# A seventh V tile kept per batch, and each head's gK in the light iteration, in an attention block's backward pass

## Chip, core and metric

One NeuronCore of a Trainium2 chip runs the kernel. The metric is device time in microseconds (us) of one execution. A NeuronCore has five engines that run their own instruction streams: TensorE (PE in the profile; its weight loads are PEld), VectorE (DVE), ScalarE (ACT), GpSimd (POOL) and SyncE (SP). They work on the on-chip memory SBUF (128 partitions) and on the accumulation memory PSUM, which has eight banks here called bank0 to bank7. Transfers between the device memory and SBUF run on 16 DMA engines; they are issued from the queues of SP, ACT and POOL.

## The reference

The reference computes one decode step of a transformer block and the gradients of all its inputs. B = 2 batches, one query each, D = 640, H = 32 heads of 128, a cache of 4096 keys and values per head, and an MLP of width 1728:

```python
q = (layernorm(x) @ wq)                       # 2 x 32 x 128
p = softmax(q . k_cache * 128**-0.5)          # 2 x 32 x 4096
o = p . v_cache
h = x + o @ wo
h2 = h + relu(layernorm(h) @ w1) @ w2
out, vjp = jax.vjp(f, x, k_cache, v_cache, wq, wo, w1, w2)
return out, *vjp(grad_out)
```

The outputs are h2 and the gradients of x, of the two caches (gK and gV, 2 x 32 x 4096 x 128 each) and of the four weight matrices. K, V, gK and gV make up nearly all of the bytes: one head of one of them is 4096 x 128 bf16, 1024 KB, and is held on chip as one tile of 8 KiB a partition.

## The kernel before

**Two passes over 64 (batch, head) pairs.** The first pass (`p1_iter`, L449) takes the pairs in order. It loads K and V of a pair, transposes K on TensorE (`pair_transpose`, L415: four groups of transposes into PSUM, each copied to a tile `t_sb` with the tag "XT"), multiplies by the query (`pair_matvec`, L431), takes the maximum (`rmax`, L559) and its negative on all partitions (`nb`, L505), the exponential (`ep`), and multiplies K by it on VectorE in two halves (`pk_half`, L461). TensorE then forms m = sum of V and pk (`m_part`) and u (`u_part`). The work is pipelined: iteration i does the scores of pair i, the exponentials of pair i-1 and the m products of pair i-2.

The second pass (`p2_iter`, L814) goes through the 64 pairs as "turns". A turn needs V again (called W there): it transposes W (T0 to T3), multiplies by the gradient of o (`dp`), forms gV = p x go on VectorE (two halves, `outer_half`, L806), and then gsp (L822) and gK = gsp x q (two halves). gV and gK are stored from POOL's queue (L871, L850). In the kernel before, a turn's last quarter of dp, its gsp and its gK are made at the start of the next turn.

**Kept V.** The order of the turns (L396) puts the last KEPT[b] heads of a batch first. The V tiles of those heads stay on chip from the first pass, so their turn needs no W load (L398). KEPT is (6, 6): 52 of the 64 turns load W.

**Phases.** The plan (L1091) interleaves the passes. Iterations 0 to 33 do pair 0 to 31 of the first pass. Then the first batch's middle (`middle_gen`, L719: the attention output, the layer norm, the MLP forward and backward, the gradient of o by `go_group`) runs in the background of iterations 34 to 40. From iteration 41 (P2_AT) to 63 the passes are mixed: every other iteration, a "mixed" one, also starts a turn; the one after it, a "light" one, finishes that turn's gV. Turns 0 to 11 are started there, 12 and 13 in iterations 64 and 65, and the rest follow alone, with the second batch's middle and the weight gradients (`fin_gen`, L955, and `gx_gen`, L989) in the background. MIXED and REST (L1139) say behind which of the eight steps of a first-pass iteration a step of the turn is issued. Background work is issued a piece at a time; `slot` says behind which steps a VectorE product of a row (`ttr`, L641) may be issued, at most one each.

**Tiles.** Twelve 8 KiB tiles (NBIG, L80) have homes: "ld" for loads, "g" for gK and gV, later "f" and "q" for the weight gradients. `take` and `give` move them, `share` sets how many each home is to have. The kept V tiles stay in "ld". Between iterations 41 and 45 three tiles move to "g". When the first pass is over its pool is released and two more tiles are added, "ld" gets KEPT[1] + 3 and "g" 5; when the second kept set is done (L1166) "ld" is cut to 5; when all gradients of o are done (`late`) six more tiles come from the space of wo. SP's queue issues the loads of K, V and W in the order of one list, written out ahead, each as soon as a tile in "ld" is free (`pump`, L1116). An instruction that needs a tile waits, on its own engine's queue, for the tile's last users.

**Small buffers that the change touches.** XT has 5 buffers, `rb` (L835) 4, `gsp` and `pp` 3. `xr`, `u4`, `fbc`, `junk` and `hbc` have a place each. The output row (`orow`, L637) has two buffers, used for two rows of the output and two of x's gradient; a row is copied by VectorE and stored from SP's queue.

Of the kernel before, what the change touches and what calls it, by code (L numbers as in the profile page):

```python
# [15 lines left out]
def kernel(  # L16
# [63 lines left out]
    NBIG = 12  # L80
# [71 lines left out]
    neg_ident = const.tile([128, 128], BF16)  # L152
    nc.vector.tensor_scalar(out=neg_ident[:], in0=ident_bf[:], scalar1=-SCALE, scalar2=None, op0=ALU.mult)
# [25 lines left out]
    xr = cols.tile([4 * ND, 128], BF16)  # L179
# [96 lines left out]
    def ln_bwd(gh, xh, rstd, add, dst, nb):  # L276

        def t3(name):
            return small.tile([128, nb, ND], FP32, tag=f"lb_{name}{nb}", bufs=1, name=f"lb_{name}")
# [3 lines left out]
        mm = small.tile([128, 2, nb], FP32, tag=f"lb_mm{nb}", bufs=1, name="lb_mm")  # L283
# [5 lines left out]
        nm = small.tile([128, 2, nb], FP32, tag=f"lb_nm{nb}", bufs=1, name="lb_nm")  # L289
# [32 lines left out]
    pkp = tc.alloc_tile_pool(name="pkp", bufs=1)  # L322
    hot = pkp.tile([128, 2 * H - 1], BF16)
    nc.gpsimd.memset(hot[:], 0.0)
    nc.gpsimd.memset(hot[:, H - 1:H], 1.0)
    es = pkp.tile([128, B, H], FP32)
# [68 lines left out]
    KEPT = (6, 6)  # L395
# [4 lines left out]
    u4 = cols.tile([128, 128], FP32)  # L400
# [14 lines left out]
    def pair_transpose(nat, g, dve=False, busy=0):  # L415
# [8 lines left out]
        t_sb = mats.tile([128, GT // 2, 128], FP32, tag="XT", bufs=5, name="t_sb")  # L424
# [24 lines left out]
    def p1_iter(i, dve_group, busy):  # L449
# [60 lines left out]
        if p is not None:  # L510
            ep = pkp.tile([128, NSC, 2], BF16, tag="ep", bufs=3, name="ep")
            nc.scalar.activation(out=ep[:], in_=p["s"][:, :, None].to_broadcast([128, NSC, 2]),  # L512
                                 func=ACT.Exp, bias=nb[:], scale=SCALE, accum_out=es[:, bp, hp:hp + 1])
# [24 lines left out]
        if p is not None and hp % OG == OG - 1:  # L538

            totp = p["bank"][:, 256:256 + OG]  # L540
            nc.tensor.matmul(totp, lhsT=half_f32, rhs=es[:, bp, hp + 1 - OG:hp + 1], start=True, stop=True)
# [66 lines left out]
    def u_out(b):  # L608

        t = pst([128, H], FP32, "mid", "uc_ps")  # L610
        nc.tensor.matmul(t[:], lhsT=u4[:], rhs=fold[:], start=True, stop=True)
        nc.vector.tensor_tensor(out=Uc[:, b, :], in0=t[:], in1=rt[:, b, :], op=ALU.mult)


# [18 lines left out]
    def store_row(col_bf, n, dst):  # L633
# [3 lines left out]
        r = small.tile([16, 128], BF16, tag="orow", bufs=2, name="orow")  # L637
# [3 lines left out]
    def ttr(in0, in1, acc, width, kc=128, junk=None):  # L641
        if junk is None:
            junk = cols.tile([128, D], BF16, tag="junk", name="junk")
# [14 lines left out]
    def go_group(b, h0, h1, hbc):  # L658
# [4 lines left out]
        for k in range(n):  # L663
            yield from turn()
            ttr(wo_t[:, h0 + k, :], hbc[:], go32[:, k:k + 1], D)
# [25 lines left out]
    def mlp_out():  # L691

        ml32 = small.tile([128, ND, B], FP32, tag="ml32", bufs=1, name="ml32")
# [16 lines left out]
        ml_bf = small.tile([128, ND, B], BF16, tag="ml_bf", bufs=1, name="ml_bf")  # L710
        nc.vector.tensor_copy(out=ml_bf[:], in_=ml32[:])
        y_bf = small.tile([128, B, ND], BF16, tag="y_bf", bufs=1, name="y_bf")
# [6 lines left out]
    def middle_gen(b):  # L719
        if o_next[0] < (b + 1) * H // OG:  # L720
            o_group()
        nc.vector.tensor_reduce(out=u4[:], in_=u_bank[0][:].rearrange("p (s d) -> p d s", s=4),
# [35 lines left out]
        FW = Dff // 3  # L758
        spread_f = bcast_cols(one(ghfc, b), NF, f_kc, fbc)
        have = 0  # L760
        for k in range(3):
            while have < min(Dff, (k + 1) * FW):
                next(spread_f)
                have += 512
# [15 lines left out]
        for h0, h1 in bounds:  # L780
            yield from go_group(b, h0, h1, hbc)
# [3 lines left out]
    def ga_gen():  # L785

        gbc = cols.tile([128, Dff], BF16, tag="fbc", name="gbc")
        for b in range(B):
            yield from bcast_cols(one(gc, b), ND, lambda c: 128, gbc[:, b * D:(b + 1) * D])
        for k in range(NW2):  # L790
# [3 lines left out]
            for c in range(k * FP, min(NF, (k + 1) * FP)):  # L794
                kc = f_kc(c)
                for b in range(B):
                    yield from turn()
                    ttr(t[0:kc, c - k * FP, :], gbc[0:kc, b * D:(b + 1) * D], ga[0:kc, b, c:c + 1], D, kc)
# [15 lines left out]
    def p2_iter(j, busy, act=0):  # L814

        c = S2[j] if j < NP1 else None
        p = S2[j - 1] if j >= 1 else None
        if p is not None:
            bp, hp = turns[j - 1]
            pair_matvec(p["dp"], p.pop("T3"), 3, gom[:, hp, bp, :, :])  # L820
            gsp = small.tile([128, NSC, 2], BF16, tag="gsp", name="gsp")
            nc.vector.scalar_tensor_tensor(  # L822
                out=gsp[:], in0=p["dp"][:, :, None].to_broadcast([128, NSC, 2]), scalar=negdot[:, hp, bp:bp + 1],
                in1=P_bf[:, bp * H + hp, :, None].to_broadcast([128, NSC, 2]), op0=ALU.add, op1=ALU.mult)
        if c is not None:
# [41 lines left out]
        yield  # L867
        outer_half(gV, c["rb"][:, 0:128], c["pp"], 1, act)
# [3 lines left out]
        give(gV)  # L872
        yield

# [114 lines left out]
    def gx_gen(fin):  # L989
# [30 lines left out]
        junk = cols.tile([128, GW], BF16, tag="fbc", name="gxj")  # L1020
        for c in range(ND):
# [4 lines left out]
            for b in range(B):  # L1026
                for k in range(NGW):
                    ttr(t[:, k * GW:(k + 1) * GW], rows[b][:, k * GW:(k + 1) * GW], gxp[:, b, c, k:k + 1], GW, junk=junk)
# [10 lines left out]
        for b in range(B):  # L1039
            gxo = small.tile([128, ND], BF16, tag="gxo", bufs=2, name="gxo")  # L1040
# [99 lines left out]
    REST = {1: 1}  # L1140
# [8 lines left out]
    for n, (i, j) in enumerate(plan):  # L1149
# [16 lines left out]
        elif fin is not None and j >= H + KEPT[1] - 1:  # L1166
            share(ld=5 + more, g=5 + 2 * more, f=3, q=2 + 3 * more)
        if j is not None:
# [4 lines left out]
            g2 = p2_iter(j, 0, 8 if i is None and j <= H else 0)  # L1173
# [32 lines left out]
        for k, _ in enumerate(p1_iter(i, i < H + 1, 0)):  # L1206
# [9 lines left out]
            if i >= P2_AT:  # L1216
                slot[0] = int(k == 6 or (k == 1 and j is None))
# [49 lines left out]
```

## Time and profile before

| | |
|---|---|
| median of 3 runs | 897.68 us (895.79 to 898.74) |
| the profiled execution | 897.56 us, of which the span of instructions is 895.8 us |
| TensorE busy | 739.5 us (83%) |
| VectorE busy | 687.7 us (77%) |
| ScalarE busy | 482.6 us (54%) |
| POOL busy | 202.7 us (23%) |
| bytes moved | 361.84 MB, mean 404 GB/s |
| largest group on VectorE | pk 128 x 1.22 us, gK 128 x 1.23 us, gV 128 x 1.14 us |

The page cuts the span into 40 slices of 22.4 us. In its lines of slices a digit is a busy share in tenths, and GB/s is what the DMA engines moved in that slice. In a row of a group, xN is the number of instructions, followed by the busy time and the mean duration in ns; behind the second bar stands the idle time of the engine just before them and what ended it. In a row of the order of time, the first number is the start in us from the span's start, the second the length, and a bracket gives the idle time before it and what ended it. Matmuls overlap, so their lengths don't add up; TensorE's busy time is no measure of how near it is to its peak.

### The profile page before, as it was taken

To read this page: it belongs to the slowest core of one execution; us is meant where nothing else is said; L and a number is where in the kernel's file an instruction comes from. 1 tells how busy PE (TensorE), PEld (TensorE's weight loads), DVE (VectorE), ACT (ScalarE), POOL (GpSimd) and SP (SyncE) were. 2 spreads that over 40 slices of the span, in tenths; PEclk is the share of its full clock that TensorE was granted. 3 is DMA by queue.
4 is the path that set the end of the run, shared out by engine and by line. 5 is a ranking of instruction groups with operands and counts; after the bars stand their busy time and mean duration, and the time that the engine had idled before them with its cause. 6 is when DMAs were issued, how large, how long until landed. Compare 5 with 4: busy or idle time off the path is not lost.

```text
span 895.8 us, 24578 instructions
## 1 busy us (share of the span) xinstructions
PE 739.5 (83%) x10145; PEld 616.0 (69%) x10145; DVE 687.7 (77%) x1284; ACT 482.6 (54%) x1242; POOL 202.7 (23%) x349
## 2 busy tenths in 40 slices
PE   4999899899997997997977776877878897787593
PEld 4888788788886886886766765665657665564452
DVE  2666788777887786786877897788788679987963
ACT  1444344344554554564645777777556864466372
POOL 1343444343211110010021232222111111111111
PEclk9999999999999899897995556555566855575555
DMA  9999999999879999999999999999999999999997
GB/s 379 425 418 416 417 406 418 425 424 380 311 307 370 377 399 424 424 424 422 399 383 400 422 419 422 419 415 421 417 417 363 425 425 425 425 425 426 425 422 295
DMA packets 56288, 361.84 MB, mean 404 GB/s; under 512 B 5680, under 2 KB 11760, under 8 KB 15472
## 3 DMA queue, kind: packets, MB, share of 16 engines
q1 hardware_dynamic: 34520, 211.13, 57.9%
q0 software_dynamic: 18432, 134.23, 35.9%
q10 hardware_dynamic: 3224, 14.92, 4.0%
q8 instruction: 80, 1.31, 0.5%
q14 instruction: 32, 0.26, 0.1%
HBM read 211.11 MB, written 149.13 MB: 402 GB/s over the span
## 4 chain that ended last, share of the span: by engine, by line
PE 42%; DMA 28%; DVE 14%; ACT 9%; issue 5%; SPq 1%; POOL 0%; ACTq 0%; POOLq 0%; DVEq 0%
PE t_ps L423 18%; DMA Vt<-in_A_v_cache_dram 13%; PE m_ps L457 10%; DMA out_dram<-gK 9%; DVE gV L809 4%; ACT gV L870 3%; PE s_ps L436 3%; PE u_ps L486 3%; ACT t_sb L428 2%; PE dp_ps L436 2%; DVE gK L809 2%; DVE pk L464 2%; PE o_ps L909 2%; DMA out_dram<-gV 2%; DVE junk L644 2%
## 5 line engine op out<-in xcount | busy, mean ns | idle before, releaser
L428 ACT COPY t_sb<-t_ps 128x512 f32<-128x512 f32 x479 | 273.6, 586 | 194.7 <-PE t_ps L423 189.7
L436 PEld LDWEIGHTS <-t_sb 128*128 128x128 bf16 x4096 | 179.4, 102 | 60.5 <-ACT t_sb L428 30.4
L423 PE MATMUL t_ps<-ident_f,Wt 128*128 128x128 f32 x832 | 197.1, 386 | 2.7 <-DMA Wt<-in_A_v_cache_dram 2.4
L457 PE MATMUL m_ps<-pk,Vt 128*128 128x129 bf16 x2048 | 171.9, 222 | 16.6 <-DMA Vt<-in_A_v_cache_dram 16.0
L464 DVE TENSOR_TENSOR pk<-Kt,ep 128x2048 bf16<-128x2048 bf16 x128 | 156.5, 1223 | 33.5 <-PE m_ps L457 15.4
L809 DVE TENSOR_TENSOR gK<-rb,gsp 128x2048 bf16<-128x2048 bf16 x128 | 152.6, 1226 | 15.3 <-DMA out_dram<-gV 13.2
L423 PE MATMUL t_ps<-ident_f,Kt 128*128 128x128 f32 x1024 | 156.0, 285 | 5.7 <-DMA Kt<-in_A_k_cache_dram 5.5
L423 PEld LDWEIGHTS t_ps<-ident_f,Wt 128*128 128x128 f32 x832 | 137.0, 200 | 32.3 <-issue 25.6
L457 PEld LDWEIGHTS <-Vt 128*128 128x128 bf16 x2048 | 125.3, 99 | 47.7 <-issue 28.9
L809 DVE TENSOR_TENSOR gV<-rb,pp 128x2048 bf16<-128x2048 bf16 (+1 forms) x128 | 142.7, 1140 | 10.2 <-DMA out_dram<-gK 8.8
L474 POOL COPY pk<-ep 128x16 bf16<-128x16 bf16 x80 | 84.1, 1053 | 160.8 <-ACT ep L512 86.5
L423 PEld LDWEIGHTS t_ps<-ident_f,Kt 128*128 128x128 f32 x1024 | 113.2, 145 | 9.8 <-PE s_ps L436 4.1
L436 PE MATMUL dp_ps<-gom,t_sb 128*128 128x2 bf16 x2048 | 95.9, 168 | 20.5 <-ACT t_sb L428 20.3
L871 POOL DMA_DIRECT2D out_dram<-gV x64 | 34.2, 534 | 293.2 <-DVE gV L809 173.5
L436 PE MATMUL s_ps<-qm,t_sb 128*128 128x2 bf16 x2048 | 87.4, 164 | 1.5 <-DVE t_sb L426 1.5
L850 POOL DMA_DIRECT2D out_dram<-gK x64 | 34.0, 531 | 227.6 <-DVE gK L809 172.6
L571 ACT CAST MT<-m_ps 128x128 bf16<-128x128 f32 x64 | 17.1, 267 | 105.3 <-PE m_ps L457 105.1
L915 ACT CAST ot<-o_ps 128x512 bf16<-128x512 f32 (+3 forms) x152 | 68.0, 492 | 6.9 <-DMA out_dram<-ot 5.6
L822 DVE SCALAR_TENSOR_TENSOR gsp<-dp_ps,negdot,P_bf 128x64 bf16<-128x64 f32 x64 | 18.0, 281 | 55.8 <-PE dp_ps L436 55.7
L836 ACT ACTIVATE rb<-dp_ps,rt 128x256 bf16<-128x256 f32 x64 | 30.2, 471 | 56.9 <-PE dp_ps L831 56.8
L644 DVE CUSTOM_DVE_ANT_0 junk<-wo_t,hbc 128x640 bf16<-128x640 bf16 x64 | 52.5, 820 | 0.2
L644 DVE CUSTOM_DVE_ANT_0 gxj<-wqs,gqr 128x1024 bf16<-128x1024 bf16 x40 | 48.8, 1219 | 1.4 <-DMA wqs<-in_A_wq_dram 1.2
(200 smaller groups left out, 763.2 us busy)
## 6 DMA issues: line engine op xcount, KB each, us to landing
Kt<-in_A_k_cache_dram SPq DMA_DIRECT2D x64, 1024.0 KB, 16.5
Vt<-in_A_v_cache_dram SPq DMA_DIRECT2D x64, 1024.0 KB, 16.0
out_dram<-gV POOLq DMA_DIRECT2D x64, 1024.0 KB, 13.5
out_dram<-gK POOLq DMA_DIRECT2D x64, 1024.0 KB, 13.7
Wt<-in_A_v_cache_dram SPq DMA_DIRECT2D x52, 1024.0 KB, 12.0
wq_t<-in_A_wq_dram SPq DMA_DIRECT2D x5, 1024.0 KB, 11.9
wo_t<-in_A_wo_dram SPq DMA_DIRECT2D x4, 1280.0 KB, 19.0
wqs<-in_A_wq_dram SPq DMA_DIRECT2D x5, 1024.0 KB, 21.0
```

The costliest lines, as they stand in the source:

```text
L423: nc.tensor.transpose(t_ps[:, j, :], natf[:, 2 * cc:2 * cc + 2, :].rearrange("p c k -> p (c k)"), ident_f[:])
L428: nc.scalar.copy(out=t_sb[:], in_=t_ps[:])
L436: nc.tensor.matmul(dst[:, sc:sc + 2], lhsT=v[:, j, :, par], rhs=vecs[:, par, :], start=(par == 0), stop=(par == 1))
L457: nc.tensor.matmul(r["m"][:, 0:129], lhsT=r["V"][:, sc, :], rhs=r["pk"][sc // HALF][:, sc % HALF, 0:129], start=(sc == 0), stop=(sc == NSC ...
L464: nc.vector.tensor_tensor(out=p["pk"][k][:, :, 0:128].rearrange("p s (a two) -> p s a two", two=2), in0=p["K"][:, sl, :].rearrange("p s (a ...
L474: nc.gpsimd.tensor_copy(out=col, in_=e)
L644: nc.vector.tensor_tensor_reduce(out=junk[0:kc, 0:width], in0=in0, in1=in1, scale=1.0, scalar=0.0, op0=ALU.mult, op1=ALU.add, accum_out=acc)
L809: nc.vector.tensor_tensor(out=pairs_view(dst[:, sl, :]), in0=row.rearrange("p (a two) -> p a two", two=2)[:, None, :, :].to_broadcast([128 ...
L836: nc.scalar.activation(out=rb[:], in_=bank[:, 128:384], func=ACT.Copy, scale=rt[:, b, h:h + 1])
L850: nc.gpsimd.dma_start(out=natural(out_2, bp, hp), in_=gK[:])
L871: nc.gpsimd.dma_start(out=natural(out_3, b, h), in_=gV[:])
L915: nc.scalar.copy(out=ot[0:P, k, n0:n0 + nn], in_=o_ps[0:P, 0:nn])
```

## The change

KEPT becomes (7, 7) and NBIG 13: 14 turns find their V on chip. The space for the thirteenth tile comes from smaller buffers: XT 5 to 4, rb 4 to 3, gsp and pp 3 to 2, orow and other late rows moved to the late pool `fin` (orow with one buffer), and one shared row `wide_row` in place of `u4`, `fbc`, `hbc`, `junk` and the other wide rows. Products whose full result isn't needed write it over P_bf's later heads, or over w1, or into the other half of the wide row. The MLP gradient's row is spread in three pieces of 640, 640 and 448 columns (before 3 x 576). In the mixed phase a turn's last quarter of dp, its gsp and its gK are made in the light iteration that follows the turn's start (`own_gK`) and no longer in the next mixed one. The background products may be issued behind step 1 of the mixed iteration instead of the light one. After the second kept set "g" gets one tile more.

The diff, cut to its core:

```diff
-    NBIG = 12
+    NBIG = 13
...
-    xr = cols.tile([4 * ND, 128], BF16)
+    xr = mats.tile([4 * ND, 128], BF16, tag="XT", bufs=4, name="xr")
...
+        lb = small if nb == 1 else fin
...
-    es = pkp.tile([128, B, H], FP32)
+    es = pkp.tile([128, 2 * OG], FP32)
...
-    KEPT = (6, 6)
+    KEPT = (7, 7)
...
-    u4 = cols.tile([128, 128], FP32)
+    u4 = [None]
...
-        t_sb = mats.tile([128, GT // 2, 128], FP32, tag="XT", bufs=5, name="t_sb")
+        t_sb = mats.tile([128, GT // 2, 128], FP32, tag="XT", bufs=4, name="t_sb")
...
+    def wide_row(name):
+        return cols.tile([128, B * D], BF16, tag="wide_row", name=name)
+
+    def later_heads():
+
+        return P_bf[:, B * H - D // NSC:, :].rearrange("p h s -> p (h s)")
+
+    def spread_some(colsrc, c0, n, kc_of, dst):
+
+        t = pst([128, D], BF16, "bc", "bcb_ps")
+        w = 0
+        for c in range(c0, c0 + n):
+            kc = kc_of(c)
+            nc.tensor.transpose(t[:, w:w + kc], colsrc[0:kc, c:c + 1].to_broadcast([kc, 128]), ident_bf[0:kc, 0:kc])
+            w += kc
+        nc.scalar.copy(out=dst[:, 0:w], in_=t[:, 0:w])
+        return w
...
-        r = small.tile([16, 128], BF16, tag="orow", bufs=2, name="orow")
+        r = fin.tile([16, 128], BF16, tag="orow", bufs=1, name="orow")
...
-        fbc = cols.tile([128, Dff], BF16, tag="fbc", name="fbc")
+        fbc = wide_row("fbc")
...
+        first_f = 0
+        for k, n in enumerate((ND, ND, NF - 2 * ND)):
+            row = fbc[:, (k % 2) * D:(k % 2 + 1) * D]
+            w = spread_some(one(ghfc, b), k * ND, n, f_kc, row)
+            yield
             for c in range(ND):
                 yield from turn()
-                ttr(w1_t[:, c, k * FW:(k + 1) * FW], fbc[:, k * FW:(k + 1) * FW], gx2p[:, c, k:k + 1], FW)
+                part = w1_t[:, c, first_f:first_f + w]
+                ttr(part, row[:, 0:w], gx2p[:, c, k:k + 1], w, part if b else later_heads())
                 yield 0.85
+            first_f += w
...
-        hbc = cols.tile([128, D], BF16, tag="rowbc", name="hbc")
-        yield from bcast_cols(one(gh1c, b), ND, lambda c: 128, hbc)
+        row = wide_row("hbc")
+        hbc, junk = row[:, 0:D], row[:, D:2 * D]
+        spread_some(one(gh1c, b), 0, ND, lambda c: 128, hbc)
+        yield
...
+    def last_dp(j, c):
+
+        b, h = turns[j]
+        pair_matvec(c["dp"], c.pop("T3"), 3, gom[:, h, b, :, :])
+
+    def score_grad(j, c):
+
+        b, h = turns[j]
+        gsp = small.tile([128, NSC, 2], BF16, tag="gsp", bufs=2, name="gsp")
+        nc.vector.scalar_tensor_tensor(
+            out=gsp[:], in0=c["dp"][:, :, None].to_broadcast([128, NSC, 2]), scalar=negdot[:, h, b:b + 1],
+            in1=P_bf[:, b * H + h, :, None].to_broadcast([128, NSC, 2]), op0=ALU.add, op1=ALU.mult)
+        return gsp
+
-    def p2_iter(j, busy, act=0):
+    def p2_iter(j, busy, act=0, own_gK=False):
 
         c = S2[j] if j < NP1 else None
-        p = S2[j - 1] if j >= 1 else None
+        p = S2.get(j - 1)
...
-            rb = mats.tile([128, 256], BF16, tag="rb", bufs=4, name="rb")
+            rb = mats.tile([128, 256], BF16, tag="rb", bufs=3, name="rb")
...
-            pp = small.tile([128, NSC, 2], BF16, tag="pp", name="pp")
+            pp = small.tile([128, NSC, 2], BF16, tag="pp", bufs=2, name="pp")
...
+        if own_gK:
+            last_dp(j, c)
         outer_half(gV, c["rb"][:, 0:128], c["pp"], 1, act)
...
         nc.gpsimd.dma_start(out=natural(out_3, b, h), in_=gV[:])
         give(gV)
-        yield
+        if own_gK:
+            gsp = score_grad(j, c)
+        yield
+        if own_gK:
+            gK = take("g", [128, NSC, 128], "gK")
+            outer_half(gK, c["rb"][:, 128:256], gsp, 0)
+            yield
+            outer_half(gK, c["rb"][:, 128:256], gsp, 1)
+            nc.gpsimd.dma_start(out=natural(out_2, b, h), in_=gK[:])
+            give(gK)
+            del S2[j]
+            yield
...
-    REST = {1: 1}
+    REST = {1: 1, 4: 1, 6: 1}
...
-            share(ld=5 + more, g=5 + 2 * more, f=3, q=2 + 3 * more)
+            share(ld=5 + more, g=6 + 2 * more, f=3, q=2 + 3 * more)
...
-            g2 = p2_iter(j, 0, 8 if i is None and j <= H else 0)
+            g2 = p2_iter(j, 0, 8 if i is None and j <= H else 0, i is not None and plan[n + 1][1] is None)
...
-                slot[0] = int(k == 6 or (k == 1 and j is None))
+                slot[0] = int(k == 6 or (k == 1 and j is not None))
```

More of the change, by code (lines that the diff above doesn't have):

```diff
@@ L322 @@
     pkp = tc.alloc_tile_pool(name="pkp", bufs=1)
+    neg_ident = pkp.tile([128, 128], BF16)
+    nc.vector.tensor_scalar(out=neg_ident[:], in0=ident_bf[:], scalar1=-SCALE, scalar2=None, op0=ALU.mult)
     hot = pkp.tile([128, 2 * H - 1], BF16)
@@ L656, in one, with go_group @@
         return src[:, :, b]
-    def go_group(b, h0, h1, hbc):
+    def go_group(b, h0, h1, hbc, junk):
         hs = slice(h0, h1)
@@ L664, in go_group @@
             yield from turn()
-            ttr(wo_t[:, h0 + k, :], hbc[:], go32[:, k:k + 1], D)
+            ttr(wo_t[:, h0 + k, :], hbc, go32[:, k:k + 1], D, junk)
             yield 0.9
@@ L691, in mlp_out @@
     def mlp_out():
-        ml32 = small.tile([128, ND, B], FP32, tag="ml32", bufs=1, name="ml32")
+        ml32 = fin.tile([128, ND, B], FP32, tag="ml32", bufs=1, name="ml32")
         nc.vector.memset(ml32[:], 0.0)
@@ L780, in middle_gen @@
         for h0, h1 in bounds:
-            yield from go_group(b, h0, h1, hbc)
+            yield from go_group(b, h0, h1, hbc, junk)
         if b > 0:
@@ L785, in ga_gen @@
     def ga_gen():
-        gbc = cols.tile([128, Dff], BF16, tag="fbc", name="gbc")
+        gbc = wide_row("gbc")
         for b in range(B):
@@ L812, in outer_half @@
             in1=colp[:, sl, None, :].to_broadcast([128, n, 64, 2]), op=ALU.mult)
-    def p2_iter(j, busy, act=0):
+    def last_dp(j, c):
[9 more added lines that the diff above has]
+    def p2_iter(j, busy, act=0, own_gK=False):
         c = S2[j] if j < NP1 else None
-        p = S2[j - 1] if j >= 1 else None
+        p = S2.get(j - 1)
         if p is not None:
             bp, hp = turns[j - 1]
[L820 to L824, printed above, removed]
+            last_dp(j - 1, p)
+            gsp = score_grad(j - 1, p)
         if c is not None:
@@ L1019, in gx_gen @@
         gxp = fin.tile([128, B, ND, NGW], FP32, tag="gxp", name="gxp")
-        junk = cols.tile([128, GW], BF16, tag="fbc", name="gxj")
+        junk = wide_row("gxj")
         for c in range(ND):
@@ L1027, in gx_gen @@
                 for k in range(NGW):
-                    ttr(t[:, k * GW:(k + 1) * GW], rows[b][:, k * GW:(k + 1) * GW], gxp[:, b, c, k:k + 1], GW, junk=junk)
+                    ttr(t[:, k * GW:(k + 1) * GW], rows[b][:, k * GW:(k + 1) * GW], gxp[:, b, c, k:k + 1], GW, junk)
                     if b == B - 1 and k == NGW - 1:
```

36 lines of the change are left out of this document (13 added, 23 removed).

## The prediction

> **What bounds the kernel now.** I read the page's slices first, then a table of busy time over stretches that I cut where the transfer rate changes, and only then the engines.
>
> ```profile
> span 895.8 us, 24578 instructions
> ...
> DMA  9999999999879999999999999999999999999997
> GB/s 379 425 418 416 417 406 418 425 424 380 311 307 370 377 399 424 424 424 422 399 383 400 422 419 422 419 415 421 417 417 363 425 425 425 425 425 426 425 422 295
> ...
> HBM read 211.11 MB, written 149.13 MB: 402 GB/s over the span
> ```
>
> Most slices stand at 415 to 425 GB/s, and none goes above 426; I take 424 as what the transfers can do here. The mean of 402 means that 5% of the span is lost at the lower slices. The stretches, with DMA share and rate in the last two columns:
>
> ```profile
> core 0: us, PE busy (x) PEld busy (x) DVE busy (x) ACT busy (x) POOL busy (x), PEclk, DMA share, GB/s
> 205.00:255.70 50.70, 48.11 (x860) 42.39 (x859) 41.75 (x119) 25.93 (x72) 13.77 (x25) 1.00 0.88 344
> 255.70:305.60 49.90, 44.59 (x709) 39.02 (x708) 38.21 (x81) 27.03 (x74) 6.15 (x8) 0.93 0.88 343
> 305.60:441.00 135.40, 121.10 (x1955) 106.43 (x1953) 106.08 (x214) 72.66 (x200) 14.16 (x24) 0.92 1.01 417
> 441.00:493.00 52.00, 39.33 (x592) 34.69 (x588) 40.91 (x84) 26.68 (x71) 9.80 (x19) 0.76 0.99 388
> 493.00:672.00 179.00, 136.81 (x1328) 110.46 (x1327) 146.04 (x258) 125.75 (x327) 45.62 (x87) 0.56 1.01 419
> 672.00:694.40 22.40, 18.17 (x202) 15.56 (x200) 18.38 (x36) 13.96 (x33) 4.39 (x9) 0.67 0.94 364
> 694.40:885.00 190.60, 147.68 (x1335) 105.97 (x1334) 154.77 (x209) 112.92 (x242) 29.10 (x63) 0.58 1.01 424
> ```
>
> From 305.6 to 441 (second half of the mixed phase) and from 493 to 885 (almost all of the second pass) the transfers are the bound: no engine is busy for more than nine tenths, the rate is 417 to 424. Between 205 and 305.6 they are not: 344 GB/s, TensorE busy for 48.11 of 50.70 us.
>
> I go by the rate, not by the share. The Trainium skill's page "Perfetto Trace Analysis", section Identifying the Most-Contended Engine, says that occupancy of the sixteen DMA engines misleads and that memory utilization should be used. The trace agrees: 441 to 493 has a share of 0.99 at only 388 GB/s. By the share alone that stretch too would count as bound; the sum would not change, since no removed load lies in it.
>
> **The change, part by part.** *Two loads of V fall away.*
>
> ```profile
> Wt<-in_A_v_cache_dram SPq DMA_DIRECT2D x52, 1024.0 KB, 12.0
> ```
>
> ```profile
> L444 SPq DMA_DIRECT2D Wt<-in_A_v_cache_dram x52: 327/328/1142, 330.8 to 823.5; - x52
> ...
> DMA to landing us min/median/max: 5.4/12.0/23.4
> ```
>
> 52 second loads for 64 turns with 12 kept become 50 with 14 kept. Each is 1024 KB = 1.0486 MB. The one of the first batch is the seventh turn's, the very first W load, issued at 330.8, inside the 417 GB/s stretch: 1.0486 MB / 417 GB/s = 2.51 us. The one of the second batch lies in the second pass, 493 to 672 at 419: 2.50 us. Together **-5.0 us**, in full only while the transfers stay the bound there. Upper end: both at 364 GB/s, the slowest row of the second pass, -5.8; lower end: none of it, 0.
>
> *The thirteenth tile.* It holds the seventh V from the first pass on, so the loads have 13 - 7 = 6 tiles where they had 12 - 6 = 6. Hence the slow stretches 205 to 305.6 and 441 to 493 stay as they are: 0. The tile is free only between the two kept sets and, after the second set, as an additional store tile; in stretches already at 417 to 424 that buys nothing. It could buy back at most what the 388 GB/s stretch lacks: 52.00 x (1 - 388/424) = 4.4 us. I take 0, since by its end the second set has filled again.
>
> *gK in the light iteration.* The two multiplies of gK, its gsp and one quarter of the dp products move from the next mixed iteration into the light one; one wo product moves the other way. Nothing is added in number; the question is whether the light iteration holds it. This is the VectorE's order in one, before, and the TensorE beside it:
>
> ```profile
> 345.46 1.22 DVE L809 TENSOR_TENSOR gV<-rb,pp 128x2048 bf16<-128x2048 bf16 x1
> 346.59 0.82 DVE L644 CUSTOM_DVE_ANT_0 junk<-wo_t,hbc 128x640 bf16<-128x640 bf16 x1
> 347.33 0.08 DVE L644 DVE_READ_ACCUMULATOR2_ANT go<- 128x1 f32 x1
> 347.33 0.29 DVE L505 TENSOR_REDUCE nb<-s_ps 128x1 f32<-128x128 f32 x1
> 347.54 1.22 DVE L809 TENSOR_TENSOR gV<-rb,pp 128x2048 bf16<-128x2048 bf16 x1
> 348.67 0.82 DVE L644 CUSTOM_DVE_ANT_0 junk<-wo_t,hbc 128x640 bf16<-128x640 bf16 x1
> 349.41 0.08 DVE L644 DVE_READ_ACCUMULATOR2_ANT go<- 128x1 f32 x1
> 349.41 1.25 DVE L464 TENSOR_TENSOR pk<-Kt,ep 128x2048 bf16<-128x2048 bf16 x1
> ...
> 350.91 1.22 DVE L464 TENSOR_TENSOR pk<-Kt,ep 128x2048 bf16<-128x2048 bf16 x1
> 352.05 0.19 DVE L559 TENSOR_REDUCE rmax<-s_ps 128x1 bf16<-128x32 f32 x1
> 352.15 0.82 DVE L644 CUSTOM_DVE_ANT_0 junk<-wo_t,hbc 128x640 bf16<-128x640 bf16 x1
> ```
>
> ```profile
> 335.80 1.07 PE L423 MATMUL t_ps<-ident_f,Kt 128*128 128x128 f32 x8
> ...
> 338.65 0.22 PE L831 MATMUL dp_ps<-ident_bf,goc 128*128 128x128 bf16 x1 [0.38 <-DVE gsp L822]
> ...
> 345.85 1.29 PE L423 MATMUL t_ps<-ident_f,Kt 128*128 128x128 f32 x8
> ...
> 352.65 0.30 PE L423 MATMUL t_ps<-ident_f,Kt 128*128 128x128 f32 x1 [1.03 <-DMA Kt<-in_A_k_cache_dram]
> ```
>
> The mixed iteration takes 345.85 - 335.80 = 10.05 us and the light one 352.65 - 345.85 = 6.80, of which 1.03 is a wait for K. VectorE never pauses in the light one. What the next iteration's TensorE needs first is rmax. Ahead of it come, new, one gK half (pitch 347.54 to 348.67 = 1.13) and gsp (a row of the same kind is 0.28), and one wo product leaves (346.59 to 347.33 = 0.74): rmax is 0.67 us later. It is wanted when the next K has had its two transposes: TensorE was ready at 352.65 - 1.03 = 351.62, the pair of transposes takes 1.07, so 352.69; rmax ended at 352.24. The slack is 0.45, the loss 0.22 us a pair. On the other side the mixed iteration loses its wait for gsp, 0.38 us. Net -0.16 us a pair, and only where TensorE is the bound, three pairs up to 305.6: nothing; I take **0**. The second gK half and the last wo product come behind rmax, where the mixed iteration (two multiplies fewer now) has room. Ends: 11 pairs x -0.38 = -4.2 and, if the light iteration becomes VectorE's, what the second rival gives.
>
> The gK store leaves POOL's queue some us earlier than before, and the following pp copy now stands behind it; pp is wanted only at the end of the mixed iteration. SP's queue is not passed by anything but the two loads that are gone.
>
> *Smaller buffers.* The transposed tiles rotate in 4 instead of 5: in the new order every tile that is overwritten has had its products an iteration earlier, because the last quarter of dp is now taken ahead of the light iteration's third transposed tile; 0. rb in 3, gsp and pp in 2: each lives for less than two turns; 0. The wide rows share one buffer but follow each other through the MLP gradient; its 15 products cover the same 1728 columns in widths 640, 640, 448; 0. All that runs from 205 to 255.7, where VectorE has 41.75 of 50.70 us, so an added wait there would not be covered.
>
> *One row buffer.* The second row of out_0 now waits, on VectorE, for the first row's store.
>
> ```profile
> L638 DVE COPY orow<-row_ps x4: 207/212/213, 783.4 to 861.2; 5x128 bf16<-5x128 bf16 x4
> ```
>
> ```profile
> 758.34 31.62 DMA out_dram<-gK
> ...
> 798.00 36.14 DMA out_dram<-gK
> ```
>
> The store goes through SP's queue, whose loads take 5.4 to 23.4 us to land, median 12.0. So VectorE may stand for some 12 us near 784, with the gV and gK multiplies queued behind it. But the stores then in flight land only 31.62 to 36.14 us after issue: the transfers have work for longer than the wait. Cost 0; without that cover, 12.
>
> *The lull.* When the second kept set is done the load tiles are cut to 5: from 9 before, from 10 after, so the preloaded turns are five, not four, and loads pause one turn longer. The pause is the 364 GB/s row; it lacks 22.40 x (1 - 364/424) = 3.2 us over four turns: **+0.8**, between 0 and 3.2.
>
> **Sum.** The profiled execution took 897.56 us: 895.8 of span and 1.8 around it; the median of the runs is 897.68, so they stand for each other. 897.6 - 5.0 + 0.8 = **893.4 us**, -0.5%.
>
> **Rivals.**
>
> *A load was hidden anyway.* If after the change the seventh turn's pair runs on TensorE: a pair before took 10.05 + 6.80 - 1.03 = 15.8 us on the engines, and a kept pair moves 6 x 1.0486 = 6.3 MB = 14.8 us at 424. So that pair can save only to 15.8, not to 14.8, unless later pairs take up the second. For: the two are close. Against: the later W pairs move 7.34 MB, 17.3 us. With half of the -5.0 lost: 896 us, within 0.3%. Chance 0.18.
>
> *The light iteration becomes VectorE's (slower).* It gets two gK halves and a gsp for one wo product: 2 x 1.13 + 0.28 - 0.74 = 1.8 us on a VectorE without a gap. If the mixed iteration can't give it back, because TensorE's m and s products wait for multiplies that come late, each pair that isn't held by W loads pays it: 7 kept turns x 1.8 = 12.6, and 893.4 + 12.6 = 906 us. It decides from a rmax delay beyond the 0.45 us of slack; to be slower than before by 0.3%, 1.0 us a pair must come through. Against: VectorE had 38.21 of 49.90 us in that stretch. Chance 0.14.
>
> *The row buffer's wait comes through:* 893.4 + 12 = 905 us, at one place, near 784. It decides when the stores in flight run out first. Chance 0.05.
>
> *Stores wait for descriptors.* The same pp copy on POOL takes from 0.25 to 1.18 us:
>
> ```profile
> L838 POOL COPY pp<-P_bf x11: 248/1177/1182, 268.1 to 439.3; 128x64 bf16<-128x64 bf16 x11
> ```
>
> ```profile
> L871 POOL DMA_DIRECT2D out_dram<-gV x48: 531/531/533, 494.3 to 881.8; - x48
> ```
>
> If a multiply can hold a copy up by 0.93 us, it may hold each of 22 stores of the mixed phase: 22 x 0.93 = 20 us of store time, of which only the 6 before 305.6 have no queue to hide in, 6 us: 899 us, within 0.3%. Against: the issue takes 531 to 533 ns whatever VectorE does. Chance 0.03. The Trainium skill's page "SBUF — State Buffer", section SBUF: two separate sides, states such a rule: VectorE and GpSimd lock a shared port for a whole instruction, and a store issued from POOL can starve for descriptors. The copy's row agrees with it, the store's row doesn't.
>
> *More than the loads:* the free tile and the better balance bring back the 4.4 us of the 388 GB/s stretch: 889 us. Chance 0.10.
>
> **How the numbers follow.** The forecast itself has 0.50. About 0.3% (2.7 us) is what a measurement of this kernel can tell from no change: below 895.0 is faster, above 900.4 slower. Forecast and last rival are faster, 0.60; the hidden load and the descriptors are the same, 0.21; the two mechanisms at 905 and 906 are slower, 0.19. The forecast's own range is 891.8 (both loads at 364 GB/s, no lull) to 895.8 (the lull at its full 3.2). The range for 8 in 10 is 890.0 to 900.0: it leaves out about half of the last rival (0.05) and, of the two slower mechanisms, what comes through nearly whole (0.15).
>
> **What would show it.** Right: 50 Wt issues and 209.0 MB read; the stretch up to the end of the first pass about 2.5 us shorter, the second pass as much again; rates still 417 to 424 there; light iterations under 7 us where no load is awaited. Wrong: TensorE waiting for rmax or pk at the head of mixed iterations; the rate in the second half of the mixed phase below 410; a VectorE gap behind the row copy near 780 followed by a dip in the rate; a deeper dip than 364 in the lull.

## The result and the profile after

The changed kernel takes 893.35 us in the median of 17 runs, the kernel before 897.66 us in 17 runs beside it. The ratio is 0.9957, with a 95% interval of 0.9942 to 0.9973: faster by 0.4%, where 893.4 was forecast. The profiled execution took 894.51 us, 892.7 of them span. The page of the changed kernel:

```profile
span 892.7 us, 24674 instructions
...
DMA  9999999999889999999999999999999999999987
GB/s 378 425 420 414 418 406 416 425 423 376 302 301 360 420 424 425 424 425 425 389 369 387 419 420 422 417 414 416 416 419 415 420 424 423 426 423 423 417 345 309
...
HBM read 209.02 MB, written 149.13 MB: 401 GB/s over the span
```

2.1 MB less are read, and yet the mean rate is 401 and not above 402: about as much time as before is lost at low slices, only elsewhere. The two slices from 291 us on, 377 and 399 before, move 420 and 424; the slice of 363 near 680 us moves 415; but the last slice but one, 422 before, moves 345 (the last moves 309, before 295). The same stretches as in the prediction, for the changed kernel; rate last:

```profile
core 0: us, PE busy (x) PEld busy (x) DVE busy (x) ACT busy (x) POOL busy (x), PEclk, DMA share, GB/s
205.00:255.70 50.70, 48.19 (x833) 42.34 (x831) 40.83 (x113) 25.69 (x68) 12.28 (x22) 0.97 0.88 332
255.70:305.60 49.90, 46.51 (x775) 40.38 (x776) 42.04 (x91) 28.98 (x79) 3.83 (x10) 1.00 0.91 360
305.60:441.00 135.40, 119.42 (x1973) 104.16 (x1970) 107.07 (x217) 75.20 (x205) 11.22 (x26) 0.97 1.01 423
441.00:493.00 52.00, 39.76 (x575) 35.46 (x573) 39.41 (x81) 25.75 (x68) 10.39 (x21) 0.70 0.95 372
493.00:672.00 179.00, 135.93 (x1342) 109.62 (x1339) 147.48 (x264) 124.70 (x320) 43.83 (x85) 0.57 1.01 418
672.00:694.40 22.40, 18.12 (x234) 15.15 (x234) 19.08 (x33) 17.14 (x33) 6.33 (x12) 0.77 1.01 415
694.40:885.00 190.60, 142.60 (x1251) 99.43 (x1250) 147.33 (x202) 108.56 (x239) 28.02 (x59) 0.58 0.97 406
```

The last row is the one to see: 406 where before had 424. Something holds the end back. VectorE's order around 773 us in the changed kernel shows a candidate:

```profile
771.04 2.36 DVE L828 TENSOR_TENSOR gV<-rb,pp 128x2048 bf16<-128x2048 bf16 x2
773.31 0.20 DVE L657 COPY orow<-row_ps 5x128 bf16<-5x128 bf16 x1
786.96 0.21 DVE L657 COPY orow<-row_ps 5x128 bf16<-5x128 bf16 x1 [13.45 <-DMA out_dram<-orow]
```

The second output row waits 13.45 us for the store of the first, out of the single buffer; 12 was the estimate. This is the gap behind the row copy that the prediction named as a sign of being wrong. The prediction gave it no cost, because stores in flight would keep the transfers busy. They did, at that place:

```profile
770.00:780.00 10.00, 5.84 (x40) 3.61 (x40) 3.52 (x5) 2.96 (x7) 0.77 (x2) 0.50 1.01 423
780.00:790.00 10.00, 4.65 (x41) 2.91 (x40) 3.01 (x6) 3.13 (x8) 0.00 (x0) 0.50 1.02 430
```

VectorE is busy for 3.0 to 3.5 of 10 us, and the rate stays at 423 to 430. But the turns and the background behind the wait come later by it. Whether the end of this execution, which is slow, pays for that, the trace alone doesn't say:

```profile
850.00:860.00 10.00, 7.80 (x68) 6.52 (x69) 6.04 (x10) 5.53 (x14) 1.56 (x4) 0.50 0.89 370
860.00:870.00 10.00, 8.67 (x72) 5.58 (x69) 6.63 (x7) 6.58 (x13) 2.25 (x6) 0.50 0.72 297
870.00:880.00 10.00, 8.91 (x60) 5.04 (x59) 4.92 (x5) 6.75 (x14) 1.17 (x3) 0.50 0.82 339
880.00:892.00 12.00, 3.77 (x25) 1.75 (x24) 2.64 (x3) 4.02 (x8) 0.53 (x1) 0.50 0.75 311
```

The light iteration does what was said of it, in the one pair looked at. VectorE's order in one, and the starts of three iterations on TensorE, in the changed kernel:

```profile
343.38 1.22 DVE L828 TENSOR_TENSOR gV<-rb,pp 128x2048 bf16<-128x2048 bf16 x1
344.52 0.82 DVE L661 CUSTOM_DVE_ANT_0 hbc<-wo_t,hbc 128x640 bf16<-128x640 bf16 x1
...
345.46 1.22 DVE L828 TENSOR_TENSOR gV<-rb,pp 128x2048 bf16<-128x2048 bf16 x1
346.59 0.28 DVE L842 SCALAR_TENSOR_TENSOR gsp<-dp_ps,negdot,P_bf 128x64 bf16<-128x64 f32 x1
346.79 1.22 DVE L465 TENSOR_TENSOR pk<-Kt,ep 128x2048 bf16<-128x2048 bf16 x1
347.92 1.22 DVE L828 TENSOR_TENSOR gK<-rb,gsp 128x2048 bf16<-128x2048 bf16 x1
...
349.21 1.22 DVE L465 TENSOR_TENSOR pk<-Kt,ep 128x2048 bf16<-128x2048 bf16 x1
350.35 0.19 DVE L560 TENSOR_REDUCE rmax<-s_ps 128x1 bf16<-128x32 f32 x1
350.45 1.22 DVE L828 TENSOR_TENSOR gK<-rb,gsp 128x2048 bf16<-128x2048 bf16 x1
```

```profile
334.69 1.07 PE L424 MATMUL t_ps<-ident_f,Kt 128*128 128x128 f32 x8
...
343.77 1.35 PE L424 MATMUL t_ps<-ident_f,Kt 128*128 128x128 f32 x8
...
349.69 1.07 PE L424 MATMUL t_ps<-ident_f,Kt 128*128 128x128 f32 x8
```

From gV's first half to the end of rmax it is 350.54 - 343.38 = 7.16 us, where it was 352.24 - 345.46 = 6.78: later by 0.38, inside the slack of 0.45 us. The mixed iteration takes 9.08 us (10.05 before), the light one 5.92 (6.80, 1.03 of them a wait for K). The wait for gsp, which stood in the mixed iterations of the kernel before,

```profile
PE dp_ps L831 <- DVE gsp L822: 4.0, 10, 0.6
```

is no longer among the changed kernel's waits in that stretch, and the one for rmax stays small:

```profile
PE m_ps L458 <- DMA Vt<-in_A_v_cache_dram: 11.5, 7, 3.4
...
PE s_ps L504 <- DVE rmax L560: 1.0, 4, 0.4
```

### The profile page after: what moved, and what is told of

Its sections match the earlier page's. It is cut to its first block, busy times and chain, and to the rows that moved or that the text cites. A ratio compares the mean times of both kernels' runs of the same rounds, so it can differ in the third digit from the quotient of the medians.

```text
span 892.7 us, 24674 instructions
## 1 busy us (share of the span) xinstructions
PE 735.6 (82%) x10145; PEld 609.4 (68%) x10145; DVE 686.0 (77%) x1284; ACT 483.6 (54%) x1238; POOL 196.0 (22%) x349
## 3 DMA queue, kind: packets, MB, share of 16 engines
HBM read 209.02 MB, written 149.13 MB: 401 GB/s over the span
## 4 chain that ended last, share of the span: by engine, by line
PE 40%; DMA 24%; DVE 18%; ACT 10%; issue 7%; SPq 0%; ACTq 0%; POOL 0%; POOLq 0%; DVEq 0%
PE t_ps L424 17%; DMA Vt<-in_A_v_cache_dram 12%; PE m_ps L458 9%; DVE gK L828 4%; DVE gxj L661 4%; DMA out_dram<-gK 3%; DVE gV L828 3%; PE s_ps L437 3%; ACT t_sb L429 3%; ACT gV L902 3%; DMA wqs<-in_A_wq_dram 3%; DMA out_dram<-ot 3%; DVE pk L465 3%; PE u_ps L487 3%; PE dp_ps L437 2%
## 5 line engine op out<-in xcount | busy, mean ns | idle before, releaser
L437 PEld LDWEIGHTS <-t_sb 128*128 128x128 bf16 x4096 | 176.7, 102 | 63.4 <-ACT t_sb L429 33.8
L424 PE MATMUL t_ps<-ident_f,Wt 128*128 128x128 f32 x800 | 188.8, 386 | 3.9 <-DMA Wt<-in_A_v_cache_dram 3.1
L424 PEld LDWEIGHTS t_ps<-ident_f,Wt 128*128 128x128 f32 x800 | 131.7, 200 | 32.9 <-issue 26.8
L880 POOL DMA_DIRECT2D out_dram<-gK x53 | 28.2, 531 | 155.8 <-DVE gK L828 131.1
L661 DVE CUSTOM_DVE_ANT_0 hbc<-wo_t,hbc 128x640 bf16<-128x640 bf16 x64 | 53.3, 833 | 0.2
```

The costliest lines, as they stand in the source:

```text
L424: nc.tensor.transpose(t_ps[:, j, :], natf[:, 2 * cc:2 * cc + 2, :].rearrange("p c k -> p (c k)"), ident_f[:])
L437: nc.tensor.matmul(dst[:, sc:sc + 2], lhsT=v[:, j, :, par], rhs=vecs[:, par, :], start=(par == 0), stop=(par == 1))
L661: nc.vector.tensor_tensor_reduce(out=junk[0:kc, 0:width], in0=in0, in1=in1, scale=1.0, scalar=0.0, op0=ALU.mult, op1=ALU.add, accum_out=acc)
L880: nc.gpsimd.dma_start(out=natural(out_2, bp, hp), in_=gK[:])
```

## The experiments

All ratios are to runs of the kernel before on the same chip (the groups e, f and g ran on different ones); intervals are 95%. "Two rows" means the row buffer of e1. Where two ratios are subtracted, the half widths are added as squares. 0.1% is 0.9 us.

**e1_two_rows: the row buffer alone undone.**

```diff
-        r = fin.tile([16, 128], BF16, tag="orow", bufs=1, name="orow")
+        k = FIN["rows"] = 1 - FIN.get("rows", 1)
+        r = FIN["gxj"][0:16, GW + 128 * k:GW + 128 * (k + 1)]
...
-        junk = wide_row("gxj")
+        junk = FIN["gxj"] = wide_row("gxj")
```

> The changed kernel, but the rows of the outputs have two buffers again (in the unused end of the wide row, since the late pool is full). In the changed kernel VectorE stands 13.4 us for the first row's store, and the last 42 us run at 297 to 370 GB/s. Theory 'the row's wait comes out at the end': the wait is gone and the tail runs near 424 GB/s until the natural fade-out of before, so 3.5 us less than the changed kernel, about 890. Rival 'the wait is hidden': 893.4, within 1 us, and a tail as slow as the changed kernel's.

Measured: 890.2 us, ratio 0.9923 (0.9899 to 0.9948). Against the changed kernel that is 0.34% less (0.05 to 0.63), 3.1 us (0.4 to 5.7), and no wait for a row's store is left. The ends can be compared only when each is counted back from its own last instruction, because e1's execution is 4 us shorter. These are the 35 us that end 8 us before the last instruction, for the kernel before, the changed one and e1:

```profile
852.80:887.80 35.00, 26.22 (x213) 17.98 (x211) 20.92 (x24) 19.66 (x38) 5.51 (x12) 0.50 1.00 419
```

```profile
849.70:884.70 35.00, 29.15 (x220) 18.89 (x220) 18.90 (x23) 22.65 (x47) 4.98 (x11) 0.50 0.81 335
```

```profile
845.70:880.70 35.00, 26.96 (x203) 17.15 (x202) 18.86 (x21) 21.30 (x43) 5.00 (x11) 0.50 0.98 408
```

With two rows the end is back at 408, close to before. (Between 850 and 885 us by the clock it is 381, but that stretch takes in more of e1's fade-out.) In this pair of kernels the single buffer cost about 3 us; e4 below tests it a second time.

**e2_light_gK_only: the new order on the kernel before.** `last_dp`, `score_grad`, `own_gK`, REST and the `slot` line as in the change; 12 tiles, 6 kept, old buffers.

```diff
-    REST = {1: 1}
+    REST = {1: 1, 4: 1, 6: 1}
...
-                slot[0] = int(k == 6 or (k == 1 and j is None))
+                slot[0] = int(k == 6 or (k == 1 and j is not None))
```

> The kernel before (12 tiles, 6 kept heads, 5 transposed tiles) with only the new order of the mixed phase: dp's last quarter, gsp and gK in the light iteration. Theory 'the bytes': the order is worth nothing, 897.7, first pass ends as before (pair 63 starts at 441). Rival 'the order': in the changed kernel the mixed phase (pairs 41 to 63) is 8.1 us shorter, the removed load explains 2.5, the order the other 5.6; so about 892 and pair 63 starts near 436. Second rival 'the order costs': 900 to 906.

Measured: 896.72 us, ratio 1.0001 (0.9973 to 1.0028). The order by itself is worth nothing, within 0.3%. What looked like a mixed phase 8.1 us shorter was a comparison of two single executions. Such positions scatter: the last u product of the first pass starts at 456.1 us in this kernel's trace and at 464.5 in g_12_66's below, and both kernels take the time of the one before.

**e3_kept_only: the change without the new place of gK.**

```diff
+            if "T3" in p:
+                last_dp(j - 1, p)
-            last_dp(j - 1, p)
...
-        if own_gK:
-            gsp = score_grad(j, c)
-        yield
-        if own_gK:
-            gK = take("g", [128, NSC, 128], "gK")
...
+        yield
...
-    REST = {1: 1, 4: 1, 6: 1}
+    REST = {1: 1}
```

> The changed kernel (13 tiles, 7 kept heads, all small buffers), but gsp and gK again at the start of the next mixed iteration, and the background product behind step 1 of the light one; only dp's last quarter stays in the light iteration, since four transposed tiles need it. Theory 'the bytes': 893.4 as the changed kernel. Rival 'the order': the mixed phase loses 5.6 us, 899. In between, the share of each is read from where pair 63 starts (441 before, 435 changed).

Measured: 895.49 us, ratio 0.9976 (0.9952 to 1.0). It lies between the two theories, 0.19% behind the changed kernel, which these intervals don't tell from nothing. It still has the single row buffer.

**e4_g5 and f_rows_g5: five store tiles after the second kept set, with one row buffer and with two.**

```diff
-            share(ld=5 + more, g=6 + 2 * more, f=3, q=2 + 3 * more)
+            share(ld=5 + more, g=5 + 2 * more, f=3, q=2 + 3 * more)
```

> The changed kernel, but after the second kept set the stores have five tiles as before and not six; the thirteenth stays with the loads. In the changed kernel the slice at 672 to 694 us moves 415 GB/s where before it moved 364. Theory 'the sixth store tile fills the lull': the slice falls back to about 364 and the time goes up by up to 3.2 us, 893.4 to 896.6. Rival 'the lull has another cause (the preloaded turns)': the slice stays above 410, 893.4.

> The two-row kernel (890.2) with five store tiles after the second kept set, the thirteenth staying with the loads. With the single row buffer that edit gave 892.7 against the changed kernel's 893.35, within the noise of both. Theory 'the sixth store tile is worth nothing where the transfers are the bound': 890.2 within 1.5 us. Rival 'one load tile more helps the tail': 887 to 888.5. Rival 'the store tile is needed once VectorE no longer stands': 892 to 893.

Measured: 892.7 us, 0.9939 (0.9916 to 0.9962), and 891.19 us, 0.9937 (0.9919 to 0.9956). Neither differs from the kernel that it was made from. The sixth store tile is not what filled the lull: without it e4's slice near 680 us moves 416.

Beside each other the two are a second test of the row buffer, and this one finds nothing: 0.02% (-0.28 to 0.32), 0.2 us (-2.5 to 2.8). Yet VectorE stands in e4 too:

```profile
783.52 0.21 DVE L657 COPY orow<-row_ps 5x128 bf16<-5x128 bf16 x1 [10.45 <-DMA out_dram<-orow]
```

And its end, counted back as above, is not slow, and no slower than with two rows:

```profile
845.40:880.40 35.00, 26.61 (x241) 17.81 (x238) 22.79 (x26) 23.17 (x47) 6.57 (x14) 0.63 0.97 400
```

```profile
845.20:880.20 35.00, 26.12 (x230) 17.72 (x227) 21.91 (x25) 22.42 (x45) 6.08 (x12) 0.60 0.95 394
```

So a wait of that length doesn't by itself make the end slow. The two tests together put the single buffer at 1.6 us (-0.2 to 3.5). Why the end is slow with six store tiles and one row stays open.

**f_kept66, f_kept76, f_kept67: thirteen tiles, other numbers of kept heads, two rows.**

```diff
-    KEPT = (7, 7)
+    KEPT = (6, 6)
```

> The two-row kernel (890.2) with 13 tiles but 6 kept heads per batch: 52 W loads again, and the thirteenth tile is a spare load tile. Theory 'the bytes': two loads of 2.5 us come back, 895.2. Rival 'the tile': the stretches that move 340 to 385 GB/s wait for load tiles, and a seventh load tile beside the kept ones (one in six more) speeds them up by up to 7 us near pair 41 to 46 and by up to 4 us near pair 60; then the spare tile is worth as much as the kept V, 888 to 891.

> The two-row kernel (890.2) with 7 kept heads in the first batch and 6 in the second: 51 W loads, the spare tile is free from the time the first set is used up. Theory 'the bytes': one load in the second pass comes back, 892.7. Rival 'the tile': one load tile more where the first pass ends (385 GB/s) gives that back, 889 to 891.

> The two-row kernel (890.2) with 6 kept heads in the first batch and 7 in the second: 51 W loads, the spare tile is a load tile through the first batch's kept turns. Theory 'the bytes': one load in the mixed phase comes back, 892.7. Rival 'the tile': pairs 41 to 46 run faster by more than 2.5 us with seven load tiles where six were, 886 to 890.

Measured: (6, 6) 891.05 us, 0.9941 (0.9926 to 0.9956); (7, 6) 892.24 us, 0.9952 (0.9935 to 0.997); (6, 7) 888.84 us, 0.9915 (0.99 to 0.993), beside (7, 7) at 0.9923. With thirteen tiles the two kept V are worth 0.18% (from -0.11 to 0.47), 1.6 us at best guess; 5 us, the theory of the bytes, is outside, since 4.2 is the most that the interval allows.

Which batch keeps the seventh does matter. (6, 7) is faster than (7, 6) by 0.37% (0.14 to 0.60), 3.3 us. The first fits its theory of the tile (886 to 890), the second its theory of the bytes (892.7). Taken over both pairs, the second batch's seventh V gives 0.28% (0.09 to 0.46), 2.5 us, as much as one load was forecast to give. The first batch's gives -0.10% (-0.28 to 0.09): there the V is worth no more than a spare load tile in its place, and a gain of 2.5 us is outside.

**g_12_66 and g_12_77: the same with twelve tiles.**

```diff
-    NBIG = 13
+    NBIG = 12
```

> The two-row kernel with 12 tiles and 6 kept heads per batch: the kernel before with the new order and the smaller buffers, no more. Theory 'the tile': 5 us slower than the same with 13 tiles (891.05), 896. Rival 'the small buffers or the order': 891 to 893, and the gain is neither the tile nor the loads.

> The two-row kernel (890.2) with 12 tiles in place of 13, 7 kept heads per batch: 50 W loads, one load tile fewer wherever a set is kept. With 13 tiles, 6 kept heads measured 891.05 and 7 measured 890.2, so the tile seems to be worth more than the loads. Theory 'the tile': without it the two saved loads are lost again in the stretches that wait for load tiles, 895 to 899. Rival 'the bytes': the loads saved count whatever the tiles, 890 to 892.

Measured: (6, 6) 898.88 us, 1.0003 (0.9979 to 1.0026); (7, 7) 918.81 us, 1.0237 (1.0209 to 1.0266). The first is near the 896 of the theory of the tile; the second goes the way of that theory, but lies 20 us above its 895 to 899. This closes the square:

| ratio, two rows | 6 kept | 7 kept |
|---|---|---|
| 12 tiles | 1.0003 | 1.0237 |
| 13 tiles | 0.9941 | 0.9923 |

A spare tile alone gives 0.62% (0.34 to 0.90), 5.6 us. Two kept V without a tile of their own cost 2.3%, 21 us. Tile and V together give 0.80% (0.46 to 1.14), 7.2 us (4.1 to 10.2). The rates say where. First 12 tiles and 6 kept:

```profile
205.00:255.70 50.70, 47.54 (x828) 42.48 (x825) 39.61 (x109) 24.28 (x66) 11.44 (x23) 0.97 0.84 317
255.70:305.60 49.90, 46.57 (x786) 40.11 (x785) 42.19 (x93) 28.94 (x79) 4.68 (x11) 1.00 0.90 358
...
435.00:493.00 58.00, 41.67 (x574) 36.62 (x571) 42.52 (x89) 25.89 (x68) 10.27 (x21) 0.77 0.95 370
```

Then 13 tiles and 6 kept, the spare tile with the loads:

```profile
205.00:255.70 50.70, 48.20 (x861) 42.57 (x859) 42.20 (x119) 25.50 (x68) 12.93 (x25) 1.00 0.93 363
255.70:305.60 49.90, 46.93 (x782) 41.17 (x783) 42.85 (x91) 31.47 (x86) 4.08 (x9) 1.00 0.92 360
...
435.00:493.00 58.00, 43.23 (x618) 39.19 (x619) 42.32 (x89) 28.36 (x75) 11.14 (x24) 0.73 0.99 394
```

And 12 tiles with 7 kept:

```profile
205.00:255.70 50.70, 46.60 (x795) 41.30 (x795) 37.96 (x105) 22.47 (x61) 12.39 (x23) 0.93 0.77 298
255.70:305.60 49.90, 40.47 (x608) 35.21 (x608) 32.88 (x78) 22.71 (x62) 3.37 (x8) 0.90 0.75 276
...
435.00:493.00 58.00, 44.66 (x673) 39.49 (x670) 40.69 (x79) 25.21 (x69) 6.12 (x15) 0.85 0.89 342
```

The tiles that hold no kept V are NBIG less KEPT: six, seven and five here, of which three move to the stores from iteration 41 on. These are single executions, and those with six differ among themselves, so all traces have to be set side by side. From 205 to 255.7 us, where the first batch's V are kept, the kernels run here move 317 to 351 GB/s with six such tiles, 355 to 367 with seven and 298 with five. From 435 to 493 us, where the second batch's V are kept, it is 370 to 391, 394 to 400 and 342. Between 255.7 and 305.6 us a seventh shows no gain (343 to 365 with six, 356 to 361 with seven), and with five the rate falls to 276. So where V is kept, one tile more raises the rate a little, and one less lowers it a lot. In the kernel with five, TensorE waits for V between 205 and 305.6 us:

```profile
PE m_ps L458 <- DMA Vt<-in_A_v_cache_dram: 9.4, 4, 4.7
```

With 12 tiles and 6 kept this wait is 1.6 us in all. The Trainium skill's page "Perfetto Trace Analysis", section Identifying Performance Opportunities, says under Optimization Strategy that consistent bubbles on the engine that should be saturated can mean that there isn't enough SBUF for the next tile. These rows agree: 298, 317 and 363 GB/s with five, six and seven tiles in the first stretch shown, 342, 370 and 394 in the last.

**g_rate_77 and g_rate_66: the background issued faster, to free the end.**

```diff
-    RATE2 = 0.65
+    RATE2 = 0.85
```

> The two-row kernel (890.2) with the weight-gradient background issued faster in the second pass (RATE2 0.85 in place of 0.65). Its last 35 us move 381 GB/s, because the last turns take 9 us each beside background that is left over. Theory 'the saved bytes are lost at the end': with the background done earlier the end runs near 420 GB/s and the time falls by (1 - 381/424) x 35 = 3.5 us, 886.7. Rival 'faster background only delays the turns': 890 or more.

> The same faster background with 13 tiles and 6 kept heads (891.05 before this edit): 52 W loads. Theory 'the saved bytes are lost at the end': once the end is bound by the transfers again, the two loads count in full, and this kernel is slower than the one with 7 kept heads by 3 to 5 us. Rival 'the loads are hidden for another reason': the two stay within 2 us of each other.

Measured: 900.1 us, 1.0032 (1.0009 to 1.0055), and 898.34 us, 1.0004 (0.9978 to 1.003). The end of the first does run near the limit, and the stretch ahead of it pays:

```profile
694.40:850.00 155.60, 127.44 (x1141) 92.90 (x1140) 129.41 (x180) 100.31 (x215) 23.96 (x49) 0.56 0.99 408
850.00:885.00 35.00, 14.40 (x184) 11.96 (x184) 24.98 (x29) 9.42 (x17) 8.79 (x15) 0.65 1.01 426
```

408 where e1 had 423 GB/s in the same stretch. The kernel with 7 kept is not faster than the one with 6 here either, where the theory had it 3 to 5 us ahead. So nothing here supports that the saved bytes are merely lost at the end. It is no clean refutation, since the faster background slowed the stretch ahead of the end.

## Why the prediction was right, point by point

The number was right, 893.4 against 893.35, and so were the sign and the main mechanism: two loads less, held in a tile of their own, with the loads' free tiles unchanged. That it is right to 0.1 us is luck: at best guess the experiments put the main term higher, and one of them finds a cost that was put at nothing, and each of these sizes is known only to a few us.

**The two loads and their tile: -5.0 forecast, 7.2 us measured (4.1 to 10.2), with both sides on two rows.** The forecast is inside the interval, and the step's equation holds: 13 - 7 load tiles beside 12 - 6. What the step did not say is how much hangs on the tile. It gave the thirteenth tile 0 and all the gain to the bytes. The square shows that the same tile left spare brings 5.6 us, that the V in it add 1.6 (not told from 0), and that the V without it cost 21. W issues fell to 50 and the bytes read to 209.02 MB, as forecast:

```profile
L445 SPq DMA_DIRECT2D Wt<-in_A_v_cache_dram x50: 327/328/1567, 343.8 to 820.3; - x50
```

Two loads that are gone for certain bring 1.6 and not 5.0 us beside a spare tile. The f kernels say where the rest is: the second batch's load shows with 2.5 us, and in the first batch a spare tile does as much as the load saved. Why there and not in the second batch stays open: the rates rise with a spare tile in both, and neither the store tile nor the rate of the background explained it.

The sign that the first pass would be 2.5 us shorter and the second as much again did not come so. The last u product of the first pass starts at 461.7 us before and 457.6 after, so what follows it got 1.0 us longer, and with two rows (457.6 of 888.7) 3.0 shorter. By the scatter of e2 such single positions prove little.

**The row buffer: 0 forecast, 3.1 us measured in one test (0.4 to 5.7), 0.2 in the other (-2.5 to 2.8).** The step was "the transfers have work for longer than the wait. Cost 0". The cover held where the wait stands (423 to 430 GB/s). What it didn't look at is the end, 70 us later: with six store tiles that was slow beside one row (335) and not beside two (408). With five store tiles no cost showed. So the cost is between nothing and some 3 us, and the path from the wait to the slow end is not shown. The rival with this mechanism gave 905 us, a cost of 12, and is out.

That 12 us was near 13.45 is partly luck. It was the median landing of a load; the row's store, issued at 773.58 us, stood behind a W load on the same queue that had been issued at 759.1 and took 27.4 us, until 786.5, and VectorE went on at 786.96. The Trainium skill's page "DMA: Bandwidth & Descriptors", section Queues, rings and completion order, says that on each DMA engine the descriptors of a queue are consumed in ring order; a row store on SP's queue then stands behind the loads. The trace agrees: 13.45 us for 1.2 KB.

**gK in the light iteration: 0 forecast, 1.0001 measured.** The slack of 0.45 us carried it: in the pair shown rmax came 0.38 us later, not 0.67. The rival of 906 us is out.

**Smaller buffers: 0 forecast.** 12 tiles and 6 kept with all of them and the new order: 1.0003; the new order without them: 1.0001.

**The lull: +0.8 forecast.** Not shown: 364 GB/s before, 415 after, where a deeper dip was the sign. In kernels with 12 tiles and 6 kept this stretch moves 364, 378 (e2) and 412 (g_12_66), so it varies without the change. No run changed the number of preloaded turns, the cause that the prediction named.

**Stores that wait for descriptors:** issues on POOL in the changed kernel are as long as before:

```profile
L903 POOL DMA_DIRECT2D out_dram<-gV x64 | 34.2, 534 | 316.9 <-DVE gsp L842 86.7
```

**A load hidden anyway, 896 us, and more than the loads, 889 us:** the first named the first batch's load, and there the kernels with thirteen tiles do show no gain over a spare tile; whether TensorE hides it, the rival's mechanism, no run separates from what the tile is worth. The time that it gave, 896, lies just above the interval of the ratio (892.5 to 895.2 us). The second wanted the stretch at 388 GB/s to run faster; in the changed kernel it moves 372. That the kernel with two rows comes near its 889 (890.2) is therefore no sign of it.

Put together, -7.2 for tile and V and +3.1 for the row make -4.1, where -5.0 and +0.8 made -4.2. The -4.1 does not confirm the two: both were taken from e1, and their sum is just the changed kernel beside 12 tiles and 6 kept, 0.46% (0.18 to 0.74).

## What to carry to other kernels

Where transfers have slack because loads wait for free tiles, a tile that is kept must bring a tile with it, and the first question for a new tile is what it is worth with nothing kept in it. When a wait is costed at nothing because transfers in flight cover it, look also at what is queued behind the waiting instruction, and test it more than once: here one test showed a cost and the other none. Compare the ends of two executions from their ends and not by the same clock times. A buffer that a store reads came free here only when the queue had got to it, small as the store was.

## What the runs showed of the hardware

A store of 1.2 KB on the queue that carries 1 MB loads held its buffer for 13.45 us in the changed kernel and for 10.45 in e4. With 12 tiles, a seventh kept V, and so one tile less for the loads, took the rate from 358 to 276 GB/s between 255.7 and 305.6 us. GpSimd's small copy ranged from 0.25 to 1.18 us before, while the issue of a store on the same engine stayed at 531 to 534 ns. Of the kernels run here, that with (6, 7) kept heads and two rows had the lowest median, 888.84 us (0.9915), not told from (7, 7) with two rows (0.9923).
